# Side loads of w2 in a DMA-bound decode step: 32 x 3 + 20 x 8 rows against 20 x 8 + 96 x 1

## Chip, cores and metric

One core of one Trainium2 chip. The metric is the time of one execution on the device in microseconds (us), as the median of several executions. Before the change it was 134.83 us in three runs (134.82 to 134.92).

## The reference, cut to what matters

```python
xn = layernorm(x)                     # x: (2, 1, 576), bf16
out = x + attention(xn) + mlp(xn)

# attention: q = xn @ wq (576 x 4096); 16 KV heads, Dh 128; the last 2048 of 8192
# positions of the K and V caches are read; softmax; o @ wo (4096 x 576)
# mlp:
h = xn @ w1 + b1                      # w1: (576, 4608)
h = relu(h) ** 2
mlp = h @ w2 + b2                     # w2: (4608, 576)
```

Two tokens meet 53.6 MB of caches and weights, each byte of which is used once. The kernel is therefore a stream of loads with some arithmetic beside it: DMA is at 9 tenths or more in 37 of 40 slices of its span.

## The kernel before

The SyncE queue loads the K and V windows, wq, w1, wo and nearly all of w2 in large loads over 128 partitions. The last 256 rows of w2 are taken out of that stream ("w2x"). ScalarE issues them early, in small parts, which are meant to fill up chosen DMA engines. Only this is touched by the change:

```python
# (rows per partition, partitions, partitions in one DMA)
XS = ((3, 32, 8), (8, 20, 5))
FT = (HW - sum(r * p for r, p, _ in XS)) // P
...
w2x_sb = [const.tile([xp, xr * D], BF16, name=f"w2x_sb_{i}") for i, (xr, xp, _) in enumerate(XS)]
const.tile([P, 24], F32, name="pad_1")
x_parts = [(s, i) for s, (_, xp, xe) in enumerate(XS) for i in range(xp // xe)]

def issue_w2x():                      # one part, called after a K or V load is issued
    if x_parts:
        s, i = x_parts.pop(0)
        xr, xp, xe = XS[s]
        rows = B_w2[FX[s]:FX[s] + xr * xp, :].rearrange("(e i r) n -> i e (r n)", e=xe, r=xr)
        tc.keep_in_program_order(nc.scalar.dma_start(out=w2x_sb[s][i:xp:xp // xe, :], in_=rows[i]))
...
def mlp_x():                          # the share of these rows in h @ w2
    i = FT
    for w, (xr, xp, _) in zip(w2x_sb, XS):
        for r in range(xr):
            out_acc(mlp["h"][0:xp, N3 + i, :], lambda a, z: w[:, r * D + a:r * D + z])
            i += 1
```

The slice `i:xp:xp // xe`: with (3, 32, 8) and (8, 20, 5) its step is 4 in both cases; part i goes to partitions i, i+4, i+8 and so on. Thus the e-th row group of each part lands in the e-th block of four partitions.

At the end of the kernel, TensorE adds the last w2 blocks as they land, a tail block (`tail_ps`) last. VectorE adds two halves (`fin_sb`), and one DMA writes the result.

Of the kernel before, what the change touches and what calls it, by code (L numbers as in the profile page):

```python
# [8 lines left out]
F32 = mybir.dt.float32  # L9
# [7 lines left out]
def kernel(  # L17
# [15 lines left out]
    P = 128  # L33
# [37 lines left out]
    HW = F // NG4  # L71
    HB = HW // 3
    FR = HW // P
    XS = ((3, 32, 8), (8, 20, 5))
    FT = (HW - sum(r * p for r, p, _ in XS)) // P
    F3 = (NG4 - 1) * HW
    CX = [(r, FT, P) for r in range(FT)]
    FX = []
    for xr, xp, _ in XS:
        FX.append(F3 + FT * P + sum(m * n for m, n, _ in XS[:len(FX)]))  # L80
        CX += [(FX[-1] - F3 + r, xr, xp) for r in range(xr)]
    assert FX[-1] + XS[-1][0] * XS[-1][1] == F
    N3 = (NG4 - 1) * FR
# [12 lines left out]
    const = ctx.enter_context(tc.tile_pool(name="const", bufs=1))  # L96
# [78 lines left out]

    const.tile([P, 96], F32, name="pad_0")
    w2x_sb = [const.tile([xp, xr * D], BF16, name=f"w2x_sb_{i}") for i, (xr, xp, _) in enumerate(XS)]
    const.tile([P, 24], F32, name="pad_1")
    x_parts = [(s, i) for s, (_, xp, xe) in enumerate(XS) for i in range(xp // xe)]

    def issue_w2x():
# [444 lines left out]
```

## Time and profile before

| | before |
|---|---|
| time, median of 3 | 134.83 us |
| span of the profiled execution | 133.0 us |
| bytes moved, mean rate | 53.74 MB, 404 GB/s |
| side loads: DMAs | 4 of 27 KB on engines 0 to 7 (8 packets of 3456 bytes each), 4 of 45 KB on engines 0 to 4 (5 packets of 9216 bytes each) |

The lines that carry the reading stand in the prediction below. Three ways of reading are used throughout.

- **The chain that ended last**, in order of time: start, length, and what the time went to.
- **Windows**: a stretch of time and its length, then the busy time of PE, PEld, DVE, ACT and POOL, each with its count, then TensorE's granted clock, the DMA share and GB/s.
- **Tracks**: the packet records name no engine. The prediction chains them into 16 tracks, one for each DMA engine. That is my working, and the naming of tracks as engines is inference from the packets they carry. The numbers are labels: engines 0 to 4 are the five tracks with packets of 9216 bytes, 5 to 7 the other three with packets of 3456 bytes, 8 to 15 the tracks with neither. Quoted is the end of the last SyncE packet on a track. Where the prediction speaks of rings that are full, it rests on the DMA row, 9 tenths or more in 37 of 40 slices; a ring slot is the time at which a load's packets start.

### The profile page before, as it was taken

What the parts mean: (1) busy time and instruction counts of PE and PEld (TensorE: products, weight loads), DVE (VectorE), ACT (ScalarE), POOL (GpSimd) and SP (SyncE); (2) the same over time, 40 slices, a digit from 0 to 9 for tenths busy, and PEclk for the clock granted to TensorE, in tenths of its full rate; (3) what the DMA queues carried; (4) which work ended last, traced back from release to release, by engine and by line L of the source; (5) the groups of instructions that cost most, each with busy time, mean ns of one, the idle gap of its engine ahead of it and who ended that gap; (6) DMA issues with size and microseconds to landing.
All of it is one profiled execution on the core that took longest, in us unless ns stands there. A gap on an engine that the chain in (4) does not pass through costs nothing.

```text
span 133.0 us, 2082 instructions
## 1 busy us (share of the span) xinstructions
PE 93.0 (70%) x850; PEld 55.1 (41%) x850; DVE 58.8 (44%) x160; ACT 46.9 (35%) x65; POOL 5.4 (4%) x18
## 2 busy tenths in 40 slices
PE   0069646988597397767798597499785477829970
PEld 0059314465363243524554353437542144215640
DVE  6724405234575436457367684527430432070010
ACT  5715403177284263346385084343320400000010
POOL 7000000010100100010010100100010000000000
PEclk9999995559999959999999999657997775555698
DMA  3999999999999999999999999999999999999940
GB/s 104 427 432 422 448 399 468 399 443 420 429 438 437 404 454 406 463 404 437 430 414 448 409 458 403 437 438 443 438 412 434 404 466 426 424 404 433 408 193 1
DMA packets 4458, 53.74 MB, mean 404 GB/s; under 512 B 551, under 2 KB 682, under 8 KB 1230
## 3 DMA queue, kind: packets, MB, share of 16 engines
q1 hardware_dynamic: 4320, 53.32, 94.5%
q10 hardware_dynamic: 130, 0.31, 0.6%
q8 instruction: 6, 0.10, 0.3%
q14 instruction: 2, 0.02, 0.0%
HBM read 53.62 MB, written 0.00 MB: 403 GB/s over the span
## 4 chain that ended last, share of the span: by engine, by line
DMA 92%; PE 4%; SPq 1%; issue 0%; DVE 0%; DVEq 0%
DMA v<-in_A_v_cache_dram 43%; DMA k<-in_A_k_cache_dram 20%; DMA w<-in_B_w_dram 17%; DMA wq<-in_A_wq_dram 12%; PE kT_ps L110 2%; PE o_ps L107 1%; SPq L128 0%; SPq L135 0%; DVE fin_sb L594 0%; PE tail_ps L107 0%; DVEq L594 0%
## 5 line engine op out<-in xcount | busy, mean ns | idle before, releaser
L110 PE MATMUL kT_ps<-ident_f,k 128*128 128x128 f32 x256 | 42.8, 315 | 11.1 <-DMA k<-in_A_k_cache_dram 7.2
L110 PEld LDWEIGHTS kT_ps<-ident_f,k 128*128 128x128 f32 x256 | 33.3, 162 | 25.9 <-issue 11.4
L327 ACT COPY kT<-kT_ps 128x1024 bf16<-128x1024 bf16 x32 | 31.8, 1013 | 22.9 <-PE kT_ps L110 22.1
L329 DVE COPY kT<-kT_ps 128x1024 bf16<-128x1024 bf16 x32 | 21.9, 684 | 16.7 <-PE kT_ps L110 16.3
L107 PE MATMUL sc_ps<-kT,qz 128*32 128x512 bf16 x128 | 10.5, 413 | 5.8 <-DVE kT L329 5.8
L107 PE MATMUL o_ps<-v,pT 128*32 128x512 bf16 x128 | 12.1, 475 | 0.0
L359 ACT ACTIVATE p<-sc_ps,bias 128x512 bf16<-128x512 f32 x8 | 5.5, 687 | 17.9 <-DVE gown L355 17.9
L588 ACT COPY part<-out_ps 17x144 f32<-17x144 f32 x2 | 0.5, 268 | 23.8 <-DVE part L588 23.8
L348 DVE TENSOR_REDUCE m<-sc_ps 128x1 f32<-128x512 f32 x8 | 5.5, 692 | 7.2 <-PE sc_ps L107 7.2
L388 DVE SCALAR_TENSOR_TENSOR o<-o_ps,in_s,o 128x128 f32<-128x128 f32 x24 | 8.3, 346 | 0.5
L362 DVE STREAM_TRANSPOSE pT<-p 128x512 bf16<-128x512 bf16 x8 | 5.7, 710 | 6.4 <-ACT p L359 6.4
L386 DVE TENSOR_SCALAR o<-o_ps,in_s 128x128 f32<-128x128 f32 x8 | 2.7, 338 | 10.8 <-PE o_ps L107 10.8
L107 PE MATMUL out_ps<-wo,ws 128*17 128x288 bf16 x64 | 6.1, 364 | 1.6 <-DVE ws L421 1.6
L352 POOL PARTITION_ALL_REDUCE gmax<-m x8 | 2.9, 365 | 91.2 <-DVE m L350 91.2
L107 PEld LDWEIGHTS <-hT_sb 128*17 128x17 bf16 (+2 forms) x104 | 4.8, 105 | 4.0 <-issue 1.3
L107 PEld LDWEIGHTS <-qz 128*32 128x32 bf16 x128 | 2.2, 98 | 10.0 <-DVE kT L329 7.4
L107 PE MATMUL op_ps<-o,of_h 128*128 128x129 f32 x16 | 4.0, 339 | 3.3 <-DVE o L388 3.2
L107 PEld LDWEIGHTS <-xnT 128*2 128x2 bf16 x100 | 2.5, 94 | 8.6 <-issue 7.5
L107 PEld LDWEIGHTS <-ws 128*17 128x17 bf16 x64 | 3.5, 111 | 3.9 <-DVE ws L421 1.9
L110 PE MATMUL pro_ps<-ident,tmp_x 2*128 2x2 bf16 x6 | 0.5, 176 | 6.6 <-DVE tmp_x L233 6.6
L107 PEld LDWEIGHTS op_ps<-o,of_h 128*128 128x128 f32 x16 | 2.8, 221 | 5.3 <-DVE o L388 5.3
L107 PE MATMUL h_ps<-w,xnT 128*2 128x384 bf16 x48 | 3.2, 419 | 2.2 <-DMA w<-in_B_w_dram 2.2
(79 smaller groups left out, 58.5 us busy)
## 6 DMA issues: line engine op xcount, KB each, us to landing
k<-in_A_k_cache_dram SPq DMA_DIRECT2D x8, 2048.0 KB, 23.6
v<-in_A_v_cache_dram SPq DMA_DIRECT2D x8, 2048.0 KB
wo<-in_A_wo_dram SPq DMA_DIRECT2D x2, 2304.0 KB
w<-in_B_w_dram SPq DMA_DIRECT2D x2, 2304.0 KB
wq<-in_A_wq_dram SPq DMA_DIRECT2D x2, 2048.0 KB, 16.2
w<-in_B_w_dram SPq DMA_DIRECT2D x3, 1296.0 KB
w_rem<-in_B_w_dram SPq DMA_DIRECT2D x1, 576.0 KB, 35.2
w<-in_B_w_dram SPq DMA_DIRECT2D x1, 576.0 KB
```

Of the source, the lines that this page charges most:

```text
L107: tc.keep_in_program_order(nc.tensor.matmul(*a, **k))
L110: tc.keep_in_program_order(nc.tensor.transpose(*a, **k))
L327: nc.scalar.copy(out=kT, in_=kT_ps[:])
L329: nc.vector.tensor_copy(out=kT, in_=kT_ps[:])
L348: nc.vector.tensor_reduce(out=m1[:], in_=sc_ps[:], axis=AX.X, op=ALU.max)
L352: nc.gpsimd.partition_all_reduce(gmax[:], m2[:], channels=P, reduce_op=ReduceOp.max)
L359: nc.scalar.activation(out=p_sb[:], in_=sc_ps[:], func=ACT.Exp, bias=bias[:, 0:1], scale=scale, accum_out=o1[:, Dh:Dh + 1])
L362: nc.vector.transpose(out=pT[:].rearrange("p j r -> p (j r)"), in_=p_sb[:])
L386: nc.vector.tensor_scalar(scalar1=in_s[:, 0:1], scalar2=None, op0=ALU.mult, **kw)
L388: nc.vector.scalar_tensor_tensor(scalar=in_s[:, k:k + 1], in1=o1[:, 0:Dh], op0=ALU.mult, op1=ALU.add, **kw)
L588: cp(out=part[32 * i:32 * i + MB, :], in_=out_ps[32 * (i // 2):32 * (i // 2) + MB, (i % 2) * OQ:(i % 2 + 1) * OQ])
```

## The change: intent and diff

The intent is to take load off the fullest engines. The 96 rows on engines 0 to 7 are to be spread over all 16, while the 160 rows on engines 0 to 4 stay.

```diff
-    XS = ((3, 32, 8), (8, 20, 5))
+    XS = ((8, 20, 5), (1, 96, 96))
...
-    const.tile([P, 24], F32, name="pad_1")
+    const.tile([P, 104], F32, name="pad_1")
```

Eight DMAs become five, the side rows need 18 matmuls instead of 22, and the order of the two kinds of part is turned round.

## The prediction

> **What bounds the kernel now.** I read the page first (busy shares, slices, queues, chain), then the chain of waits in order of time, the table of windows over the tail, the timeline of PE at the end, and last the records of single DMA packets that lie under the DMA slices. DMA is at 9 tenths in every slice but the first and the last two, and the chain that ended last is 92% DMA:
>
> ```profile
> span 133.0 us, 2082 instructions
> ...
> DMA  3999999999999999999999999999999999999940
> ...
> q1 hardware_dynamic: 4320, 53.32, 94.5%
> q10 hardware_dynamic: 130, 0.31, 0.6%
> q8 instruction: 6, 0.10, 0.3%
> q14 instruction: 2, 0.02, 0.0%
> ...
> DMA 92%; PE 4%; SPq 1%; issue 0%; DVE 0%; DVEq 0%
> ```
>
> The reader is to see that q1 (loads issued by SyncE) fills the engines, and that all that the change touches is in q10 (issued by ScalarE), 0.31 MB. The chain in order of time says how it ends:
>
> ```profile
> 107.61 22.06 DMA w<-in_B_w_dram
> 129.66 0.04 issue
> 129.70 0.27 PE tail_ps L107 x4
> 129.97 0.03 DVEq L594
> 130.00 0.05 issue
> 130.05 0.31 DVE fin_sb L594
> ```
>
> The last w2 load was issued at 107.6 us and landed 22 us later; its first packet started at 126.2. It queued behind earlier loads, so the end is set by bytes and packets per DMA engine, on the slowest of 16. PE is the near second. In the windows (length, busy time of PE, PEld, DVE, ACT, POOL, then granted clock, DMA share, GB/s) and in PE's timeline:
>
> ```profile
> 120.00:125.00 5.00, 4.96 (x42) 2.85 (x44) 0.00 (x0) 0.00 (x0) 0.00 (x0) 0.50 1.01 427
> 125.00:130.00 5.00, 4.21 (x76) 2.63 (x70) 0.59 (x2) 0.54 (x2) 0.00 (x0) 0.96 0.59 236
> ```
>
> ```profile
> 127.24 1.27 PE L107 MATMUL out_ps<-w,hT_sb 128*17 128x288 bf16 x18 [0.27 <-DMA w<-in_B_w_dram]
> 128.62 0.43 PE L107 MATMUL tail_ps<-w,hT_sb 128*17 128x144 bf16 x16
> 129.32 0.62 PE L107 MATMUL tail_ps<-w,hT_sb 128*17 128x144 bf16 x12 [0.28 <-DMA w<-in_B_w_dram]
> ```
>
> PE is full from 120 to 125 at half clock, and waits for data by only 0.27 us at 127.2 and 0.28 us near the end: DMA is the bound there, with little to spare.
>
> [...]each 27 KB part shows as 8 packets of 3456 bytes and each 45 KB part as 5 of 9216 bytes, each engine adding one 4-byte semaphore write. [...]q10's packets stand between q1's, and push these back. [...]
>
> **The sixteen engines apart.** Packet records name no engine, but a packet starts 3 to 6 ns before the previous one of its engine ends, so all 4,400 chain into 16 tracks, and the tracks with 9216-byte packets are engines 0 to 4. This is my inference. From the chains, start to next start: 1152 bytes 47 ns, 3456 bytes 131, 9216 bytes 344, 16384 bytes 607, a semaphore write 6. That is about 4.7 ns a packet plus 27 bytes a ns, so small packets cost little. The tracks end their last q1 packet at (us):
>
> - engines 0 to 4 (four parts of 3456 and four of 9216): 128.60, 128.64, 128.65, 129.18, 129.36. The last two each also carried one 8192-byte instruction fetch (q14).
> - engines 5 to 7 (four of 3456): 127.27, 128.65, 128.68, the last two with a 16 KB instruction fetch (q8), which costs an engine some 1.4 us.
> - engines 8 to 15 (nothing of w2x): 126.59, 126.82, 126.84, 126.96, and with a q8 fetch 128.13, 128.16, 128.20, 128.21.
>
> Check: 4x131 + 4x344 + 8x6 = 1948 ns for engines 0 to 4 over a bare one, 126.8 + 1.95 = 128.75 against 128.6 measured.
>
> **The change part by part.** (a) *Removed*: the four parts of 96 rows on engines 0 to 7, 4x131 + 4x6 = 548 ns on each. (b) *Kept, earlier*: the 160 rows on engines 0 to 4, same packets, at 1.4 to 45 us where they stood at 45 to 60; the rings are full throughout, so the place does not matter. (c) *Added*: 96 packets of 1152 bytes, six an engine, 6x47 + 6 = 288 ns on each of 16. (d) Net: engines 0 to 7 lose 548 - 288 = 260 ns, engines 8 to 15 gain 288. New ends: 128.34 to 128.39, 128.92, **129.10** for 0 to 4; 128.42 at most for 5 to 7; 128.50 at most for 8 to 15. The maximum moves 129.36 -> 129.10, by -0.26 us, and the same engine stays last. (e) PE: two transposes of some 56 ns and four matmuls of 128 ns (2.81 us for 22) go, about 0.6 us, between 106.8 and 114.2 us. This lies ahead of the last PV block, not at the end; it gives PE room in the tail and moves nothing that DMA sets. (f) Issue: three DMAs fewer on ScalarE, so the semaphores of SyncE's DMAs rotate differently. In the order of instructions one early V load waits for the second wq load (landed 18.27 us) where it was issued at 13.45; its ring slot comes at some 33 us. The later loads wait for loads that landed 10 us or more before their slots; nothing starves. (g) The padding changes so that the large tiles move by exactly 2048 bytes a partition: I give it nothing.
>
> Sum: -0.26 us at the last landing, matched at the end if PE keeps its 0.34 us from landing to the last matmuls: 134.83 - 0.26 = **134.57 us**, rounded to 134.6, or 0.2% faster.
>
> **The rivals.** *A, engines 8 to 15 become last.* They gain 0.29 us, and if the end were theirs, 135.1. Against: they end 1.15 us before the last one. For it only if the w2x share cost more than its bytes. *B, the instruction fetches move.* The end belongs to two engines with a q14 fetch. [...]if q14 left engines 0 to 4 the maximum would be 128.50, -0.86 us, 134.0; if a 16 KB fetch came onto one of them, 128.39 + 1.4 = 129.8, +0.4 us, 135.3. Against: both fetches come early, at 32 and 64 us, and three runs agree within 0.1 us, so the place looks fixed; this is the weakest point. *C, PE's clock.* PE starts the last wo block some 0.5 us earlier, and if the clock is freed later than at 125.4, where it was, the 18 + 28 last matmuls at half clock end up to 2 us later: 135 to 136.5. [...]If freed earlier, PE waits for DMA and nothing changes. *D, hidden anyway*: if the last landing did not move because the HBM start-up scatter (the undisturbed engines differ by 0.37 us) falls otherwise, 134.8.
>
> **Range and chances.** 134.6 is the sum; D and scatter of the engines make 134.4 to 134.9 usual; B widens both ends, C the upper: 134.1 to 135.1 for 8 in 10. Two per cent is 2.7 us, three times what the most favourable case gives; only C at its worst approaches it. Faster by over 2%: 0.01; same: 0.97; slower: 0.02.
>
> **What would show it.** Right: q10 with as many bytes, 20 packets of 9216 and 96 of 1152; last landing near 129.4 in the chain, last tail matmuls near 129.4; tracks of engines 0 to 4 still last, 8 to 15 at 128.5 at most; PE's wait before the third w2 block over 0.27 us. Wrong: the last track one of 8 to 15 (A); a fetch on another class of tracks (B); granted clock 0.50 after 125.4 and no DMA wait before the tail (C); any gap in the DMA slices before 125 (f).

## The result and the profile after

| | before | after |
|---|---|---|
| time, median (range) of 4 runs each | 134.88 us (134.82 to 134.93) | 134.68 us (134.54 to 134.75) |
| ratio, 95% interval | | 0.9984 (0.9967 to 1.0001) |
| five more rounds | 134.88 us (9 runs) | 134.72 us (134.61 to 134.81, 5 runs) |
| their ratio, 95% interval | | 0.9988 (0.9976 to 1.0001) |

A ratio is the mean time of one kernel's runs over that of the other's of the same rounds, so it is not quite the ratio of the medians. Executions over 1.5% slower than the fastest of the same kernel are left out of the means. The two ratios make -0.22 us and -0.16 us of 134.88 us; -0.26 had been predicted. Each interval by itself just reaches 1.

From the page of the kernel after: its span, its DMA row in 40 slices, the packet total, the queue of ScalarE (packets, MB, share of 16 engines) and the chain by engine.

```profile
span 132.9 us, 2067 instructions
...
DMA  3999999999999999999999999999999999999950
...
DMA packets 4506, 53.74 MB, mean 404 GB/s; under 512 B 535, under 2 KB 762, under 8 KB 1278
...
q10 hardware_dynamic: 178, 0.31, 0.6%
...
DMA 76%; PE 13%; DVE 4%; ACT 2%; issue 1%; SPq 1%; POOL 1%; DVEq 0%; ACTq 0%; POOLq 0%
```

The same bytes are moved in 48 more packets, all of them in q10 (130 before), and there is still no gap in the DMA row. The 96 packets of 1152 bytes stand on all 16 tracks, six each on 14 of them (8 and 4 on the other two, where the chaining may have crossed); that they would was an estimate of mine in step (c). The chain's DMA share fell from 92% to 76%. That is no finding: the chain, followed back, wandered through TensorE work in the first 70 us, where DMA is full in either kernel. Its end, which counts, is the same. In order of time, kernel after:

```profile
107.54 22.07 DMA w<-in_B_w_dram
129.65 0.27 PE tail_ps L107 x4
130.00 0.31 DVE fin_sb L594
```

The two windows over the tail of the kernel after, and TensorE's timeline there (start, length, what; in brackets the idle time before, and what ended it):

```profile
120.00:125.00 5.00, 4.85 (x48) 3.06 (x50) 0.10 (x1) 0.00 (x0) 0.00 (x0) 0.59 1.01 429
125.00:130.00 5.00, 3.65 (x70) 2.28 (x64) 0.59 (x3) 0.54 (x2) 0.00 (x0) 1.00 0.61 242
```

```profile
127.20 1.27 PE L107 MATMUL out_ps<-w,hT_sb 128*17 128x288 bf16 x18 [0.80 <-DMA w<-in_B_w_dram]
128.59 0.43 PE L107 MATMUL tail_ps<-w,hT_sb 128*17 128x144 bf16 x16
129.28 0.62 PE L107 MATMUL tail_ps<-w,hT_sb 128*17 128x144 bf16 x12 [0.27 <-DMA w<-in_B_w_dram]
```

The last four tail matmuls start 0.05 us earlier than before (129.65 against 129.70). The wait for the third w2 block grew from 0.27 to 0.80 us: TensorE has more room, DMA has not. The tracks end as follows (us).

| engines | before | after, predicted | after, measured |
|---|---|---|---|
| 0 to 4, no instruction fetch | 128.60, 128.64, 128.65 | 128.34 to 128.39 | 128.24, 128.34, 128.34 |
| 0 to 4, with an 8 KB fetch | 129.18, 129.36 | 128.92, 129.10 | 129.01, 129.31 |
| all others, at most | 128.68 | 128.50 | 128.54 |

The five engines 0 to 4 ended 0.24 us earlier in the mean. The last of them, which sets the end, gained only 0.05 us in this execution. That execution took 134.73 us, the second slowest of its four; the profiled execution before took 134.84 us. Of the 0.11 us between these two, 0.05 come from the last track and 0.06 from after the arithmetic: from the end of `fin_sb` to the end of the span 2.63 us pass instead of 2.69.

### The profile page after: what moved, and what is told of

The parts are those of the page before. It is cut to its first block, busy times and chain, and to the rows that moved or that the text cites.

```text
span 132.9 us, 2067 instructions
## 1 busy us (share of the span) xinstructions
PE 87.5 (66%) x844; PEld 51.7 (39%) x844; DVE 58.5 (44%) x160; ACT 46.9 (35%) x65; POOL 5.4 (4%) x18
## 4 chain that ended last, share of the span: by engine, by line
DMA 76%; PE 13%; DVE 4%; ACT 2%; issue 1%; SPq 1%; POOL 1%; DVEq 0%; ACTq 0%; POOLq 0%
DMA v<-in_A_v_cache_dram 28%; DMA k<-in_A_k_cache_dram 18%; DMA w<-in_B_w_dram 17%; DMA wq<-in_A_wq_dram 12%; PE kT_ps L110 6%; PE sc_ps L107 3%; PE q_ps L107 2%; ACT kT L327 1%; PE o_ps L107 1%; DVE m L348 1%; DVE qrow L293 1%; DMA w2x_sb<-in_B_w_dram 1%; ACT p L359 1%; POOL gmax L352 1%; DVE kT L329 1%
## 5 line engine op out<-in xcount | busy, mean ns | idle before, releaser
L110 PE MATMUL kT_ps<-ident_f,k 128*128 128x128 f32 x256 | 39.4, 297 | 12.5 <-DMA k<-in_A_k_cache_dram 7.9
L110 PEld LDWEIGHTS kT_ps<-ident_f,k 128*128 128x128 f32 x256 | 30.4, 151 | 26.3 <-issue 10.3
L107 PE MATMUL sc_ps<-kT,qz 128*32 128x512 bf16 x128 | 9.7, 384 | 5.8 <-DVE kT L329 5.8
L107 PEld LDWEIGHTS <-hT_sb 128*17 128x17 bf16 (+2 forms) x100 | 4.2, 98 | 4.2 <-issue 2.3
L453 DVE TENSOR_TENSOR hrow<-t 98x384 bf16<-98x384 f32 x3 | 1.6, 556 | 8.3 <-ACT t L452 8.2
L107 PE MATMUL q_ps<-wq,xnT 128*2 128x512 bf16 x32 | 2.9, 499 | 3.5 <-DMA wq<-in_A_wq_dram 3.5
```

The lines of the kernel that those rows point to most:

```text
L107: tc.keep_in_program_order(nc.tensor.matmul(*a, **k))
L110: tc.keep_in_program_order(nc.tensor.transpose(*a, **k))
L453: nc.vector.tensor_tensor(out=hrow[:, k * HB:(k + 1) * HB], in0=t1, in1=t1, op=ALU.mult)
```

## The experiments

Twelve kernels were run. The theory was the prediction's: the engine with the most packet time sets the end, and only bytes and packets count. Its rivals were: TensorE sets it; the order of the parts does it; the place in SBUF matters.

### part_first: the order of the two kinds of part

```diff
-    XS = ((8, 20, 5), (1, 96, 96))
+    XS = ((1, 96, 96), (8, 20, 5))
```

> The changed kernel's two parts in the order of the kernel before: the 96 single rows first, then the 160. Bytes per engine as in the changed kernel. Theory (bytes per engine): 134.6 to 134.7, ratio 0.998 to 0.999. Theory P: a small stall shared by the tracks at the 96-row part, now at 5 to 10 us[...]: 134.55 to 134.9. Rival (the large parts issued first are what helped): 134.85.

Measured: 134.63 us (134.53 to 134.67, 5 runs; before 134.85), ratio 0.9984 (0.9970 to 0.9998). The last track ended at 129.08 us; 129.10 was the prediction's number. The changed kernel's tracks show a stretch at 53 to 54.5 us, while the 96-row part runs, in which all 16 fall behind by 0.08 us (0.14 us in the repeat). Here I found no such stretch. So the sum of packets met the landing to 0.02 us where no stall intervened; as start-up scatter moves tracks by more than that, so close a match is partly luck. The changed kernel's shortfall lies partly in that shared stall. In time the two kernels can't be told apart: 134.63 us against 134.68 and 134.72, from different jobs.

### order_swap: the order alone

```diff
-    XS = ((3, 32, 8), (8, 20, 5))
+    XS = ((8, 20, 5), (3, 32, 8))
```

> The same parts as the kernel before (160 rows on engines 0 to 4, 96 rows on engines 0 to 7), only issued in the order of the changed kernel: the 160 rows first. Theory (the fullest DMA engine sets the end, bytes per engine alone count): each engine carries what it carried before, last track at 129.2 to 129.5, so 134.8 us, ratio to before 0.999 to 1.001. Rival (the earlier place of the large packets is what helped): some 134.65, ratio 0.9985.

Measured: 134.99 us (134.91 to 135.12, 4 runs; before 134.86), ratio 1.0009 (0.9996 to 1.0022). The last track ended at 129.66 us, later than expected (129.2 to 129.5). The order alone gains nothing.

### changed_again: the changed kernel once more

> The changed kernel once more, in five rounds, for a narrower interval. By the account of bytes per engine less a shared stall of some 0.08 us at the 96-row part: 134.6 to 134.7 us, ratio 0.998 to 0.999; the upper end of the interval under 1.

Measured: 134.72 us, ratio 0.9988, as in the table above. The upper end of the interval is 1.0001, not under 1 as expected. The last tracks ended at 129.12 and 129.28 us, the same two with the 8 KB fetches. The fetches stay where they were. The engines 0 to 4 ended 0.17 us earlier than before in the mean, the last one 0.08 us; the last of the others ended at 128.93 us.

### no_x_matmuls: is it TensorE?

The changed kernel without the side rows' matmuls; its result is wrong.

```diff
     pv_all(NU - 2)
-    mlp_x()
     pv_all(NU - 1)
```

> The changed kernel without the 18 matmuls that use the 256 rows (wrong result on purpose; all loads stay), some 2.4 us of PE work between 112 and 114.5 us. Theory (DMA sets the end, PE's work there is hidden): 134.6 to 134.7 us, ratio 0.998 to 0.999 like the changed kernel. Rival (PE is the path in the tail, and the change gains through its fewer matmuls): 132.5 to 134 us.

Measured: 134.66 us (134.57 to 134.78, 5 runs), ratio to before 0.9986 (0.9974 to 0.9999). TensorE's timeline at the third w2 block, and the chain's end:

```profile
127.13 1.27 PE L107 MATMUL out_ps<-w,hT_sb 128*17 128x288 bf16 x18 [1.60 <-DMA w<-in_B_w_dram]
```

```profile
107.48 22.08 DMA w<-in_B_w_dram
129.60 0.27 PE tail_ps L107 x4
```

All 18 matmuls are gone, the wait for data grows from 0.80 to 1.60 us, and the end stays within 0.05 us of the changed kernel's. TensorE is not what sets the time, so the four matmuls that the change saves can't be the gain.

### no_loads: what all side loads cost

The changed kernel with a memset in place of the five loads; its result is wrong.

```diff
-            rows = B_w2[FX[s]:FX[s] + xr * xp, :].rearrange("(e i r) n -> i e (r n)", e=xe, r=xr)
-            tc.keep_in_program_order(nc.scalar.dma_start(out=w2x_sb[s][i:xp:xp // xe, :], in_=rows[i]))
+            if i == 0:
+                nc.gpsimd.memset(w2x_sb[s][:], 0.0)
```

> The changed kernel with the 256 rows not loaded at all (the tiles are cleared instead; wrong result on purpose): what the rows cost in all. Theory (fullest engine): all engines bare, those with a 16 KB fetch end at 128.2 and are last, those with the small fetch at 127.4, so the last is 1.16 us under before: 133.6 to 133.8 us, ratio 0.991 to 0.992. Rival (the loads are hidden): 134.6 or more.

Measured: 133.70 us (133.62 to 133.88, 4 runs; before 134.88), ratio 0.9913 (0.9900 to 0.9927). The last track ended at 128.22 us against 128.2 expected. The side loads, hidden among large ones and issued early, cost 1.0 us of the changed kernel (134.72 us in the same job). A small load is not free here, where the engines never idle: the last track ends 1.06 us earlier without them.

### spread_all: all 256 rows over all engines

```diff
-    XS = ((3, 32, 8), (8, 20, 5))
+    XS = ((1, 128, 128), (1, 128, 128))
...
-    const.tile([P, 24], F32, name="pad_1")
+    const.tile([P, 2176], F32, name="pad_1")
```

> All 256 rows as one row to each of 128 partitions, twice, so 16 packets of 1152 bytes on every engine (2 x (8 x 47 + 6) = 764 ns on each) and nothing extra on engines 0 to 4. Theory (fullest engine): engines 0 to 4 fall by 1948 - 764 = 1184 ns to 128.2 at most; the last becomes one of the engines with a 16 KB instruction fetch, 128.2 + 0.76 = 128.97; that is 0.39 us under before: 134.4 to 134.5 us, ratio 0.997. Rival (small packets cost much more than their bytes, or something else than DMA engines sets the end): no faster than the changed kernel, 134.65 or more.

Measured: 134.78 us (134.76 to 134.86, 4 runs; before 134.86), ratio 0.9994 (0.9981 to 1.0006). The last track ended at 129.10 us (expected 128.97). It was now one of those with a 16 KB fetch, as expected; the two with the 8 KB fetch ended at 128.01 and 128.30. The last landing moved by -0.26 us, the time by only -0.08. The end of the chain:

```profile
107.36 22.07 DMA w<-in_B_w_dram
129.47 0.27 PE tail_ps L107 x4
```

The tail matmuls do start 0.23 us earlier than before. From the end of `fin_sb` to the end of the span, however, 2.84 us pass instead of 2.69, so the time came out where the rival had it (134.65 us or more). The trace shows where this loss arises. SyncE closes each of these kernels with five waits for semaphores at one line. Before, the wait for the output's DMA is the third of them; here it is the first, and lasts 24.2 us instead of 8.0. So four waits instead of two follow the landing of the result, at 0.06 us each. Up to that landing 1.77 us pass in both kernels, after it 1.07 us instead of 0.92. In `own_ports` below it is the second, three waits follow, and 2.75 us pass.

### mix: a finer balance, and a miss

```diff
-    XS = ((3, 32, 8), (8, 20, 5))
+    XS = ((8, 10, 5), (1, 128, 128), (1, 48, 48))
...
-    const.tile([P, 24], F32, name="pad_1")
+    const.tile([P, 320], F32, name="pad_1")
```

(The loop that copies the columns of `hb` was made to take any number of entries, here and in the two kernels below that need it.)

> 80 rows as eight to each of 10 partitions on engines 0 to 4 (two parts, 700 ns each engine) and 176 rows as one to a partition on all engines (11 packets, 529 ns each). Theory: engines 1 to 3 with the small fetch end at 129.36 - 1.948 + 0.70 + 0.53 = 128.64, engines with a 16 KB fetch at 128.2 + 0.53 = 128.73, so the last is 0.63 us under before: 134.2 us, ratio 0.995. Rival (end not set by these engines): 134.6 or more.

Measured: 134.91, 135.04, 135.62 and 135.70 us, and two slow runs of 138.32 and 140.07; ratio of the fast ones 1.0032 (1.0013 to 1.0052). The theory of bytes and packets had promised a gain and failed. In the profiled run all 16 tracks fell behind together at 9.7 to 10.8 us, by 0.3 to 0.4 us, and at 41 to 42 us, by 0.13 us. Both are stretches in which a side part was under way: the second part of the 80 rows, and the 48 rows. While the 128-row part ran, from 31.4 to 36.8 us, they did not. With 10 partitions and 5 per DMA the slice's step is 2, and only the 128-row part covers all partitions as the large loads do. From what the last runs below show I put the difference down to the place; in this kernel that was not tested. Why the runs scatter so widely I can't say.

### four_engines: the miss made large

```diff
-    XS = ((3, 32, 8), (8, 20, 5))
+    XS = ((8, 32, 4),)
...
-    const.tile([P, 24], F32, name="pad_1")
+    const.tile([P, 400], F32, name="pad_1")
```

> All 256 rows as eight to each of 32 partitions, eight parts of four partitions, so all on engines 0 to 3 (8 x 350 = 2800 ns each) and none elsewhere: the overload taken on purpose. Theory: the last of engines 1 to 3 ends at 129.36 - 1.948 + 2.80 = 130.21, +0.85 us: 135.7 us, ratio 1.006. Rival (w2x transfers are hidden, the end comes from PE or the total bytes): 134.8, ratio 1.000.

Measured: 137.78 us (137.60 to 138.02, 4 runs; before 134.86), ratio 1.0216 (1.0203 to 1.0229): +2.9 us where +0.85 was expected. The end of the chain:

```profile
110.40 22.06 DMA w<-in_B_w_dram
132.50 0.27 PE tail_ps L107 x4
```

An excess on the four engines was foreseen. Not foreseen: engines that carry nothing of w2x end at 127.75 to 128.2 us instead of some 126.8. All 16 tracks stall together at each part, 1.1 to 1.2 us in all. With 32 partitions and 4 per DMA the slice's step is 8, so the e-th row group lands in every second block of four partitions, not in the e-th. That suggested the next three.

### contig, dst_only, src_only: where a part is written

All three are the kernel before, with the same rows per partition, the same packets and the same engines. `contig` reads adjoining row groups and writes adjoining partitions, and its result is correct. `dst_only` changes only where a part is written, `src_only` only where it is read; their results are wrong.

```diff
# contig: both lines; src_only: the first; dst_only: the second
-            rows = B_w2[FX[s]:FX[s] + xr * xp, :].rearrange("(e i r) n -> i e (r n)", e=xe, r=xr)
+            rows = B_w2[FX[s]:FX[s] + xr * xp, :].rearrange("(i e r) n -> i e (r n)", e=xe, r=xr)
-            tc.keep_in_program_order(nc.scalar.dma_start(out=w2x_sb[s][i:xp:xp // xe, :], in_=rows[i]))
+            tc.keep_in_program_order(nc.scalar.dma_start(out=w2x_sb[s][i * xe:(i + 1) * xe, :], in_=rows[i]))
```

> The kernel before with one thing altered: each part of w2x fills adjoining partitions (part i, engine e: partition 5i + e or 8i + e) in place of every fourth (4e + i). Same bytes, packets, engines, order and result. Theory P ([...]all 16 tracks stall together for 0.07 to 0.4 us, as they did at the 96-row part of the changed kernel and at each part of the four-engine run): stalls on all tracks at most of the eight parts, in all 0.4 to 1.2 us, so 135.3 to 136.1 us, ratio 1.003 to 1.009. Rival B (only bytes per engine count): 134.85, ratio 0.999 to 1.001, no stall shared by the tracks.

> The kernel before, each part of w2x read from the same rows as there but written to adjoining partitions (part i, engine e: partition 5i + e or 8i + e); the rows then stand in the wrong partitions, so the result is wrong on purpose. It separates the two things that the run contig altered at once. Theory S (the place written in SBUF makes the shared stalls): like contig, 137 to 138 us, ratio 1.015 to 1.024. Rival H (reading adjoining rows of HBM at the same time makes them): 134.85, ratio 1.000.

> The kernel before, each part of w2x written to every fourth partition as there, but read from adjoining rows; wrong result on purpose. Theory S: 134.85, ratio 0.999 to 1.001, no stall shared by the tracks. Rival H: like contig, 137 to 138 us.

| | time (4 runs each) | ratio, 95% interval |
|---|---|---|
| contig | 137.48 us (137.19 to 138.10) | 1.0201 (1.0179 to 1.0223) |
| dst_only | 137.49 us (137.34 to 137.67) | 1.0192 (1.0177 to 1.0208) |
| src_only | 134.90 us (134.84 to 134.97) | 1.0001 (0.9987 to 1.0014) |

`dst_only` and `src_only` came out as the theory of the place had it. `contig` had been expected at 135.3 to 136.1 us: right in kind, and less than half of the size.

Windows from 12 to 70 us, in which six of the eight parts run; the last figure is GB/s. First the kernel before:

```profile
12.00:70.00 58.00, 44.14 (x374) 25.96 (x372) 28.31 (x64) 26.86 (x38) 1.82 (x5) 0.88 1.01 431
```

Then `contig`, `dst_only` and `src_only`, one fence each:

```profile
12.00:70.00 58.00, 40.52 (x342) 24.93 (x340) 26.33 (x58) 24.45 (x34) 1.83 (x5) 0.90 1.01 418
```

```profile
12.00:70.00 58.00, 42.15 (x340) 25.09 (x339) 25.88 (x57) 23.98 (x33) 1.47 (x4) 0.85 1.01 419
```

```profile
12.00:70.00 58.00, 44.09 (x374) 25.44 (x372) 28.39 (x65) 26.98 (x38) 1.83 (x5) 0.88 1.01 430
```

The DMA share stays at 1.01 in all four, while the GB/s falls from 431 to 418 and 419: a packet that takes longer counts as busy for longer, and only the GB/s shows the loss. 431 to 418 GB/s over 58 us is a loss of some 1.7 us of the stream. The packet total on the page of `contig` shows that nothing was cut up differently; it is that of the kernel before, 4458 packets, at a lower rate:

```profile
DMA packets 4458, 53.74 MB, mean 396 GB/s; under 512 B 551, under 2 KB 682, under 8 KB 1230
```

In `contig`, engines without any side load fall behind by 1.2 us in four stretches of 0.08 to 0.54 us, and some 9216-byte packets take 527 to 772 ns instead of 347. So the cost lies in the destination alone (ratio 1.0192 in `dst_only`, 1.0001 in `src_only`), and it reaches engines that have no part in the load.

So far the runs carry it: with the step of four no stretch shows in which all tracks fall behind (in the kernel before, the only packets after 10 us that take over 15 ns more than usual are, the fetches' own aside, eight single ones beside the eight instruction fetches), and the adjoining placement costs 2% (1.0201 and 1.0192). Why it costs that, no record shows.

### own_ports: the two findings together

The engines with spare time get more, and the two large side parts are placed as in the runs above in which no shared stall showed: 120 rows on engines 0 to 4 with a step of 4, as in the kernel before, and 128 over all partitions, as in `mix`. The last 8 rows, meant for one engine, go to partitions 0 to 3.

```diff
-    XS = ((3, 32, 8), (8, 20, 5))
+    XS = ((6, 20, 5), (1, 128, 128), (2, 4, 1))
...
-    const.tile([P, 24], F32, name="pad_1")
+    const.tile([P, 104], F32, name="pad_1")
```

> 128 rows as one to each of 128 partitions[...], 120 rows as six to each of 20 partitions, every fourth, on engines 0 to 4, eight rows on engine 0. Theory P plus bytes: no stall shared by the tracks; engines 1 to 3 with the small fetch end at 129.36 - 1.948 + 4 x (258 + 6) ns + 0.38 = 128.85, engines with a 16 KB fetch at 128.2 + 0.38 = 128.6, so the last is 0.5 us under before: 134.3 to 134.4 us, ratio 0.996. Rival B alone predicts the same here. If neither holds: 134.7 or more.

Measured, with a correct result: 134.40 us (134.34 to 134.54, 5 runs; before 134.85), ratio 0.9968 (0.9956 to 0.9981). The last track ended at 128.96 us, against 128.85 expected, with no shared stall: while its 128-row part ran, at 49 to 55 us, no track fell behind by more than 0.01 us. The changed kernel's 96-row part ran at 51 to 56 us with fewer packets of the same size, and did stall the tracks. The end of its chain:

```profile
107.19 22.09 DMA w<-in_B_w_dram
129.32 0.27 PE tail_ps L107 x4
```

The tail starts 0.38 us earlier than in the kernel before. This version beats both kernels, by 0.32% against before. Against the changed kernel the comparison is of runs of different jobs: 134.40 against 134.68 and 134.72. It alters balance and place at once, so what each of them gained is not shown.

## Why the prediction was right or wrong, point by point

- **The bound: right. The sum: too large.** The fullest engine sets the end, and the same two tracks stay last. The mean of the engines 0 to 4 moved by -0.24 and -0.17 us in the two profiles, but the last track, which counts, by -0.05 and -0.08 instead of -0.26. The time moved by -0.16 to -0.22 us; the whole -0.26 was in the forecast of 134.57. That the time came nearer to the forecast than the last track did is luck in part: 0.06 us of it came from after `fin_sb`. `part_first` has the forecast landing, 129.08 against 129.10. `no_loads` confirms the scale: 1.0 us for all side loads.
- **What fell short: step (c).** The 96 packets were costed by their bytes and number alone, 288 ns an engine. The runs add a shared stall of 0.08 to 0.14 us on all 16 tracks while that part is under way, and more on the last one. Chained again, with the order of SyncE's 270 packets a track as a further condition, the last track comes apart as follows (us; "start-up" is the time it had lost by 10 us, "stall" what it lost at 51 to 57 us):

| | start-up | stall | sum: -0.26, change of start-up, stall | last track against before |
|---|---|---|---|---|
| before | 0.57 | 0.00 | | 129.36 |
| changed kernel | 0.65 | 0.14 | -0.04 | -0.05 |
| `changed_again` | 0.53 | 0.21 | -0.09 | -0.08 |
| `no_x_matmuls` | 0.61 | 0.12 | -0.10 | -0.11 |
| `part_first` | 0.55 | 0.00 | -0.28 | -0.28 |

So the stall and the scatter of the start-up account for the shortfall. In the changed kernel's trace, 20 of the 16 KB packets that start at 52.9 to 54.5 us take 38 to 80 ns over their usual 611; in the kernel before, none there does. As to the cause of the stall, I think it is the placement, as the 96 rows fill the adjoining partitions 0 to 95; that is a guess. Small packets as such don't do it, nor does a part that fills all 128 partitions: in `own_ports` no track fell behind by more than 0.01 us. The effect of the placement is shown in `dst_only` (1.0192); that it is the same effect at this size is not shown. `part_first`, with the same part at 5 to 8 us, shows no stall that can be told from start-up scatter, which moves a track by up to 1 us in the first 10 us (in the kernel before, the first 16 KB packets, at 2.1 to 2.4 us, take 0.27 to 0.78 us over the usual 0.61).

- **Step (b), the place in time: right in the main.** Order alone (`order_swap`) gave 1.0009 with an interval about 1. For the 96-row part the place in time may matter, as `part_first` suggests.
- **Step (e), TensorE: wrong in size, without effect.** The last wo block was to come 0.5 us earlier, and came 0.11 us later (120.15 against 120.04). The granted clock was 0.50 from 100.2 us on instead of from 108.3, and a PV block at 107.8 took 1.90 us instead of 1.37. The wait before the third w2 block grew as foretold, but not because TensorE started earlier: the granted clock was 1.00 again at 124.1 us instead of 125.4, and the 36 matmuls before that wait took 2.44 us instead of 3.12. `no_x_matmuls` shows that none of it reaches the end.
- **Steps (f) and (g): right as far as seen.** A V load was issued later, as foretold (18.66 us instead of 13.45), and there is no gap in the DMA row. That its packets start at some 33 us was an estimate: 13.1 MB of loads were issued before it, which at the mean 404 GB/s take 32.4 us. No run changes the padding alone, so that it has no effect is not shown.
- **Rival A** (engines 8 to 15 last): not seen, 128.54 at most in the first profile and 128.93 in the repeat. Its condition, "if the w2x share cost more than its bytes", is what `contig` and `four_engines` made true.
- **Rival B** (fetches move): not seen in two profiles of the changed kernel. In this kernel the fetches do cost time on the side of the loads: a 16 KB one costs the DMA engine that carries it some 1.4 us (in the kernel before its own packet takes 0.88 to 0.96 us, and a packet beside it some 0.5 us more than usual), the two 8 KB ones 0.56 and 0.84 us before the change, and in both kernels the two tracks that end last carried a fetch. What the time would be without them was not tried. **Rival C** (clock later): the granted clock rose to 1.00 earlier, at 124.1 us; what decides when it rises is not shown. **Rival D** (hidden by scatter): it describes the profiled run by itself, where the last track gained 0.05 us, but not the two sets of runs.

## What to carry to other kernels

Where DMA never idles, as here (9 tenths or more in 37 of 40 slices), add up packet time for each DMA engine, instruction fetches included, and trim the fullest one; the busy share, 1.01 over 12 to 70 us in the kernel before, does not tell which it is. Try where in SBUF a small side load is written: every fourth partition showed no shared stall here, and with the same bytes and packets the adjoining partitions cost 2% (137.49 us against 134.88), some six times the 0.32% that the best version gained. Look at GB/s in windows rather than at DMA busy time: the share was 1.01 at 431 and at 418 GB/s.
